# Low weight bits added as integers on GpSimd, and the gain of w_out multiplied there

## The chip, the cores and the metric

The kernel runs on one core of a Trainium2 chip. Its time is the device time of one execution in microseconds (us). Before the change three runs gave 670.62, 671.80 and 671.99 us, median 671.8 us. One more execution was taken with a profile; it took 670.49 us, of which the traced span is 668.7 us.

## The reference

Two stages follow each other. The first is a linear attention over 8 batches with 8 heads of 576 tokens and 64 columns; the second is a feed-forward block over 4608 tokens with 512 columns and 1024 hidden columns.

```
phi(x) = concat(exp(p - m), exp(m - p)),  p = x @ w_phi,  m = max |p| over features
num = phi(q) @ (phi(k)^T v);   den = phi(q) . sum(phi(k));   x = num / (den + 1e-6)
h = x @ w_in;  solu = h * softmax(h);  ln = (solu - mean) / sqrt(var + 1e-6) * g_ln
out = ln @ w_out
```

The inputs w_in (512 x 1024) and w_out (1024 x 512) arrive as 64-bit floats, the others as 32-bit floats.

## The kernel before

Attention runs over 16 units: a unit `u` is one batch and one half of its heads, and it has two parts (`sub`), each a pair of heads. Of a unit, TensorE projects keys (`pjk`) and queries (`pjq`), the middle tokens of both (`pjm`), VectorE takes the row maxima (`m`) and subtracts them (`dk`, `dq`), ScalarE takes both exponentials (`ek`, `fq`), TensorE forms the key-value product (`kvT`), the numerator (`num`) and the denominator (`den`), VectorE makes the reciprocal (`cmr`), and DMAs spread it over the partitions (`rb<-d`). GpSimd multiplies the numerator by it (`xa`, `xb`). For the first two units TensorE turns the queries (`dT`); for later units VectorE and two DMAs do.

The feed-forward block runs over 36 tiles of 128 tokens. The activations and the weights are split into a high and a low part, so that each product is three matmuls: `h` from `mxh`, `mxl` and `win_h`, `win_l` (24 matmuls of 512 columns a tile), and `o` from `uhs`, `uls` and `w_out_h`, `w_out_l` (24 more). GpSimd makes the low parts by subtraction.

The weights need work before that. There are eight weight tiles `i` of 128 x 1024: 0 to 3 are w_in, 4 to 7 are w_out. A tile comes from memory as pairs of 32-bit words (`wraw`, low and high word, 1 MB). `w_rebias` (ScalarE) puts the exponent of the high word in range. `w_bits` step 0 (VectorE) shifts the high word left by three into the 32-bit float `w`; step 1 (VectorE) shifts the low word right by 29 and ors its three bits in. For w_in, ScalarE then copies `win_h` and GpSimd subtracts to give `win_l`. For w_out, `w_gain` (ScalarE, two instructions a tile) multiplies by a column of g_ln, TensorE sums the tiles (`cmean`, then `cmall`), and GpSimd and ScalarE take the mean off and split the result (`w<-w,cms`, `w_out_h`, `w_out_l`).

No `h` matmul can start before all four `win_l` are there, and `cmean` needs all four gains of w_out. Both stand in TensorE's order within a few instructions of each other: `cmean`, one `pjk`, one `pjq`, `cmall`, and then the first `h`.

The order of all work is written out: `SEQUENCE` is a list of operation numbers, and every engine issues its share of it in that order, each with its own queue. An instruction that waits holds back all that stands behind it on its engine. The buffers (SBUF tags and eight PSUM banks, six of them single under tag `a`) are given out in the same order. The profile shows nearly all instructions under one helper line, so they are told apart by the names of their tiles.

Of the kernel before, what the change touches and what calls it, by code (L numbers as in the profile page):

```python
# [8 lines left out]
U32 = mybir.dt.uint32  # L9
AF = mybir.ActivationFunctionType  # L10
ALU = mybir.AluOpType
# [14 lines left out]
KV_PE = (0, 1)  # L26
SWITCH = 165.0
# [1285 lines left out]
```

## Time and profile before

| | before |
|---|---|
| median of three runs | 671.8 us |
| profiled execution | 670.49 us |
| its span | 668.7 us |
| TensorE (PE) busy | 660.4 us, 99% |
| VectorE (DVE) busy | 491.6 us, 74% |
| ScalarE (ACT) busy | 370.3 us, 55% |
| GpSimd (POOL) busy | 394.6 us, 59% |
| DMA, mean rate | 202 GB/s |

The shares are means over the whole span. The weights are prepared in its first 70 us, and there the engines stand otherwise: VectorE and the DMA engines are nearly full and GpSimd is mostly idle. The page's busy time of PE also holds short waits inside a matmul's modelled end, so the waits of PE are read from the view of waits and from start times in the timeline. PE's granted clock is 1.00 over the span but for its last stretch.

### The profile page before, as it was taken

How to read it: one execution, taken by the hardware profiler on the slowest of the kernel's cores; microseconds unless marked ns; L12 is line 12 of the kernel's file. 1: busy time of each engine (PE TensorE's matmuls, PEld its weight loads, DVE VectorE, ACT ScalarE, POOL GpSimd, SP SyncE). 2: the span in 40 equal slices, each digit the busy share in tenths (PEclk: the TensorE clock that was granted, in tenths of full speed). 3: DMA queues.
4: the chain of work that ended last, by engine and by line, in shares of the span. 5: the costliest groups of instructions: out<-in, count | busy, mean ns of one | idle time of the engine just before them, and what ended most of it. 6: DMA issues, size and time to landing. Idle time of an engine off the chain costs nothing.

```text
span 668.7 us, 13163 instructions
## 1 busy us (share of the span) xinstructions
PE 660.4 (99%) x4932; PEld 493.9 (74%) x4932; DVE 491.6 (74%) x754; ACT 370.3 (55%) x717; POOL 394.6 (59%) x438
## 2 busy tenths in 40 slices
PE   8999999999999999999999999999999899999998
PEld 6776667677777777777768777787777677788887
DVE  6999888878987697797788888589675746533440
ACT  4888874566465565455664576364545563331322
POOL 0125998786675574677593955845857555554501
PEclk9999999999999999999999999999999999999999
DMA  7897888777765695887685667764874663532302
GB/s 269 303 310 230 277 215 237 220 223 243 243 192 185 217 292 191 238 260 221 191 262 158 202 210 215 263 189 124 259 218 144 213 206 92 183 113 85 104 16 80
DMA packets 131280, 135.31 MB, mean 202 GB/s; under 512 B 55568, under 2 KB 105104, under 8 KB 130704
## 3 DMA queue, kind: packets, MB, share of 16 engines
q1 hardware_dynamic: 131216, 134.46, 65.1%
q8 instruction: 39, 0.64, 0.4%
q14 instruction: 25, 0.20, 0.1%
HBM read 85.53 MB, written 48.91 MB: 201 GB/s over the span
## 4 chain that ended last, share of the span: by engine, by line
PE 86%; DVE 9%; DMA 2%; issue 1%; POOL 1%; ACT 0%; SPq 0%; DVEq 0%; POOLq 0%; ACTq 0%
PE o L258 29%; PE h L258 28%; PE kvT L258 11%; PE num L258 6%; PE pjq L258 4%; PE pjk L258 4%; PE den L258 3%; DVE m L258 2%; DVE dq L258 2%; DVE w L258 2%; DVE dk L258 1%; PE pjm L258 1%; DMA out<-os 1%; DMA rb<-d 1%; DVE dE L258 0%
## 5 line engine op out<-in xcount | busy, mean ns | idle before, releaser
L258 POOL TENSOR_TENSOR uls<-uTs,uhs 128x1024 fp32r<-128x1024 f32 x33 | 78.9, 2391 | 46.4 <-ACT uhs L258 34.9
L258 PE MATMUL o<-w_out_h,uhs 128*128 128x512 f32 x264 | 103.9, 393 | 0.0
L258 PE MATMUL o<-w_out_h,uls 128*128 128x512 f32 x264 | 102.8, 389 | 0.0
L258 PE MATMUL o<-w_out_l,uhs 128*128 128x512 f32 x264 | 102.8, 389 | 0.0
L258 ACT ACTIVATE ek<-dk 128x512 f32<-128x512 f32 (+1 forms) x160 | 88.8, 587 | 18.8 <-DVE dk L258 15.5
L258 POOL TENSOR_TENSOR zt<-ek 128x512 f32<-128x512 f32 x52 | 68.2, 1311 | 48.8 <-ACT ek L258 48.3
L258 PE MATMUL h<-win_h,mxh 128*128 128x512 f32 x288 | 91.9, 400 | 0.0
L258 ACT ACTIVATE fq<-pT 128x512 f32<-128x512 f32 (+1 forms) x140 | 74.1, 561 | 31.6 <-DMA pT<-dqd 21.3
L258 PE MATMUL h<-win_h,mxl 128*128 128x512 f32 x288 | 89.0, 390 | 0.5 <-POOL mxl L258 0.5
L258 PE MATMUL h<-win_l,mxh 128*128 128x512 f32 x288 | 89.0, 390 | 0.0
L258 DVE TENSOR_REDUCE nm<-h 128x1 f32<-128x1024 f32 x36 | 43.8, 1218 | 60.0 <-PE h L258 60.0
L258 ACT ACTIVATE eu<-h,nm 128x1024 f32<-128x1024 f32 x36 | 40.1, 1113 | 59.9 <-DVE nm L258 52.3
L258 PEld LDWEIGHTS h<-win_h,mxh 128*128 128x128 f32 x288 | 52.0, 188 | 15.4 <-issue 1.4
L258 PEld LDWEIGHTS h<-win_h,mxl 128*128 128x128 f32 x288 | 54.0, 188 | 12.4 <-POOL mxl L258 0.9
L258 PEld LDWEIGHTS h<-win_l,mxh 128*128 128x128 f32 x288 | 54.1, 188 | 11.6
L258 PE MATMUL kvT<-ek,rawv 128*64 128x256 f32 x512 | 62.0, 383 | 0.0
L258 DVE SCALAR_TENSOR_TENSOR qz<-fq,kvf,qz 128x576 f32<-128x576 f32 x46 | 44.2, 972 | 21.1 <-ACT qz L258 21.1
L258 PEld LDWEIGHTS o<-w_out_h,uhs 128*128 128x128 f32 x264 | 49.6, 188 | 11.7 <-issue 0.5
L258 PEld LDWEIGHTS o<-w_out_h,uls 128*128 128x128 f32 x264 | 49.6, 188 | 10.4
L258 PEld LDWEIGHTS o<-w_out_l,uhs 128*128 128x128 f32 x264 | 49.6, 188 | 10.0
L258 PE MATMUL num<-fq,kvf 128*64 128x448 f32 (+1 forms) x304 | 56.5, 499 | 0.0
L258 ACT ACTIVATE qz<-fq,kvf 128x576 f32<-128x576 f32 x46 | 34.6, 770 | 38.2 <-DMA kvf<-dk 38.2
(109 smaller groups left out, 1278.1 us busy)
## 6 DMA issues: line engine op xcount, KB each, us to landing
du<-ub SPq DMA_DIRECT2D x33, 512.0 KB, 3.9
uTs<-du SPq DMA_DIRECT2D x33, 512.0 KB, 5.2
rb<-d SPq DMA_DIRECT2D x64, 144.0 KB, 3.9
dqd<-dq SPq DMA_DIRECT2D x14, 640.0 KB, 4.9
pT<-dqd SPq DMA_DIRECT2D x14, 640.0 KB, 5.9
out<-os SPq DMA_DIRECT2D x35, 256.0 KB, 4.1
rawq<-in_q SPq DMA_DIRECT2D x32, 256.0 KB, 4.2
rawk<-in_k SPq DMA_DIRECT2D x32, 256.0 KB, 5.0
```

The costliest lines, as they stand in the source:

```text
L258: return self.tc.keep_in_program_order(method(*args, **kwargs))
```

## The change

Three operations on the weights move, and the order of everything is new.

- The low bits are prepared apart from the float. For tiles 0 to 3 GpSimd takes the top byte of the low word, scales it by 1/32, limits it, and writes a whole number of 0 to 7 over the low word (`TENSOR_SCALAR wraw`). For tiles 4 to 7 VectorE shifts the low word right by 29 in place (`TENSOR_SCALAR wraw`). Neither needs the rebias of ScalarE.
- GpSimd adds that number to `w` as 32-bit integers (`TENSOR_TENSOR w<-w,wraw`, all eight tiles). VectorE's fused shift-and-or is gone.
- GpSimd multiplies w_out by the column of g_ln (`TENSOR_SCALAR w<-w,gcol`, two a tile). ScalarE's two multiplications a tile are gone.

```diff
+U8 = mybir.dt.uint8
+LOW_POOL = (0, 1, 2, 3)
 SEQUENCE = (
-    122, 2, 1, 123, 77, 124, 126, 125, 79, 86, 84, 312, 93, 127, 82, 80, 134, 88, 94, 83, 128, 87, 140, 137, 81,
...
     def w_bits(i, step, tag):
         raw = W["raw", i]
         lo, hi = raw[:, :, 0], raw[:, :, 1]
-        if step == 0:
+        if step == "hi":
             W[i] = sb(tag, [P, DF], U32, f"w32_{i}")
             nc.vector.tensor_scalar(out=W[i], in0=hi, scalar1=3, scalar2=None, op0=ALU.logical_shift_left)
+        elif step == "lo":
+            if i in LOW_POOL:
+                nc.gpsimd.tensor_scalar(
+                    out=lo, in0=lo.bitcast(U8)[:, :, 3], scalar1=1.0 / 32, scalar2=7.484375, op0=ALU.mult, op1=ALU.min
+                )
+            else:
+                nc.vector.tensor_scalar(out=lo, in0=lo, scalar1=29, scalar2=None, op0=ALU.logical_shift_right)
         else:
-            nc.vector.scalar_tensor_tensor(
-                out=W[i], in0=lo, scalar=29, in1=W[i], op0=ALU.logical_shift_right, op1=ALU.bitwise_or
-            )
+            nc.gpsimd.tensor_tensor(out=W[i], in0=W[i], in1=lo, op=ALU.add)
...
     def w_gain(i):
...
-            nc.scalar.activation(out=w, in_=w, func=AF.Copy, scale=gcol[:, f : f + 1])
+            nc.gpsimd.tensor_scalar(out=w, in0=w, scalar1=gcol[:, f : f + 1], scalar2=None, op0=ALU.mult)
```

On GpSimd all of the new work stands before the first `mxl`, the low part that the first `h` needs. Before, this is all that GpSimd had from the end of its set-up to that point:

```order
L258 TENSOR_TENSOR win_l<-w_0_490,win_h 128x1024
L258 TENSOR_TENSOR xa<-E,rb 128x576
L258 TENSOR_TENSOR win_l<-w_1_431,win_h 128x1024
L258 TENSOR_TENSOR xa<-E,rb 128x576 x2
L258 TENSOR_TENSOR win_l<-w_3_760,win_h 128x1024
L258 TENSOR_TENSOR xa<-E,rb 128x576
L258 TENSOR_TENSOR win_l<-w_2_995,win_h 128x1024
L258 TENSOR_TENSOR mxl<-xa,mxh 128x512
```

After the change, these are the last twelve rows of the same stretch, with twelve more ahead of them (of the numbers in the names, the first is the weight tile):

```order
L261 TENSOR_SCALAR wraw_609<-wraw_609 128x1024
L261 TENSOR_TENSOR w_6_776<-w_6_776,wraw_542 128x1024
L261 TENSOR_TENSOR xa<-E,rb 128x576
L261 TENSOR_TENSOR w_2_811<-w_2_811,wraw_609 128x1024
L261 TENSOR_TENSOR xa<-E,rb 128x576
L261 TENSOR_TENSOR w_5_910<-w_5_910,wraw_626 128x1024
L261 TENSOR_TENSOR win_l<-w_3_661,win_h 128x1024
L261 TENSOR_SCALAR w_5_910<-w_5_910,gcol 128x512 x2
L261 TENSOR_SCALAR w_6_776<-w_6_776,gcol 128x512 x2
L261 TENSOR_TENSOR xa<-E,rb 128x576 x2
L261 TENSOR_TENSOR win_l<-w_2_811,win_h 128x1024
L261 TENSOR_TENSOR mxl<-xa,mxh 128x512
```

The conversion and the add that the last `win_l` needs, and the gains that `cmean` needs, now stand in GpSimd's queue among the four `xa`.

VectorE starts the program in another order. Before, its first rows behind the memset were these (`m<-pjq`, `dq` are the first query group, whose two `dq` feed the first two `dT` of TensorE):

```order
L258 TENSOR_REDUCE m<-pjq 128x4 x2
L258 TENSOR_TENSOR dq<-pjq,m 128x512 x2
L258 TENSOR_REDUCE m<-pjk 128x4 x2
L258 TENSOR_TENSOR dk<-pjk,m 128x512 x2
L258 TENSOR_REDUCE m<-pjm 128x2 x2
```

Now, behind one `m<-pjq`, they are:

```order
L261 TENSOR_TENSOR dq<-pjq,m 128x512
L261 TENSOR_REDUCE m<-pjq 128x4
L261 TENSOR_REDUCE m<-pjk 128x4 x2
L261 TENSOR_TENSOR dk<-pjk,m 128x512 x2
L261 TENSOR_REDUCE m<-pjm 128x2
L261 TENSOR_TENSOR dk<-pjm,m 128x128
L261 TENSOR_TENSOR dqm<-pjm,m 128x128
L261 TENSOR_REDUCE m<-pjm 128x2
L261 TENSOR_REDUCE m<-pjk 128x4
L261 TENSOR_TENSOR dk<-pjm,m 128x128
L261 TENSOR_REDUCE m<-pjk 128x4
L261 TENSOR_TENSOR dq<-pjq,m 128x512
```

The first `dq` moved ahead of the second `m<-pjq`, and the second `dq` moved behind the key group and the middle tokens.

ScalarE casts the first `win_h` earlier. Before, the cast stood here, behind work of the second unit:

```order
L258 ACTIVATE fq<-dT 128x512
L258 ACTIVATE ek<-dk 128x4x128
L258 ACTIVATE fq<-dT 128x2x64 x2
L258 COPY E<-num 128x288
L258 CAST win_h<-w_1_431 128x1024
```

Now it stands right behind the first `kvf`, ahead of the middle queries of the first unit:

```order
L261 ACTIVATE wraw_240<-wraw_240 128x1024
L261 COPY kvs<-kvT 128x384
L261 ACTIVATE fq<-dT 128x512 x2
L261 COPY kvf<-kvt 128x384
L261 CAST win_h<-w_0_315 128x1024
```

The cast reads `w` as GpSimd's add leaves it, and the last `fq` that the first `den` needs stand behind it. TensorE's matmuls are the same in number and kind, 3380 of them in the program, and the same set of them stands ahead of the first `h`; only their order differs.

## Rows read from the trace of the kernel before

**Rows 1.** The page, busy time and share of each engine.
```profile
PE 660.4 (99%) x4932; PEld 493.9 (74%) x4932; DVE 491.6 (74%) x754; ACT 370.3 (55%) x717; POOL 394.6 (59%) x438
```

**Rows 2.** Waits of PE, whole span: total us, times, longest us.
```profile
PE den L258 <- DVE qz L258: 2.0, 1, 2.0
...
PE dT L258 <- DVE dq L258: 1.1, 1, 1.1
PE h L258 <- POOL mxl L258: 0.5, 1, 0.5
```

**Rows 3.** Two stretches: length, busy PE, PEld, DVE, ACT, POOL, clock, DMA share, GB/s.
```profile
10.00:55.00 45.00, 45.00 (x614) 32.24 (x610) 44.30 (x80) 38.55 (x78) 8.02 (x4) 1.00 0.92 310
55.00:70.00 15.00, 14.30 (x186) 8.83 (x185) 14.93 (x26) 12.11 (x21) 9.20 (x6) 1.00 0.78 228
```

**Rows 4.** Chain that ended last, first 75 us: start, us, what.
```profile
8.57 1.20 DVE m L258 x2
...
10.97 0.66 DVE m L258 x2
11.63 0.20 DVE dqm L258
...
56.05 4.60 DMA rb<-d
...
68.24 1.26 POOL mxl L258
```

**Rows 5.** Timeline, first 70 us: start, us, engine, operation, idle before.
```profile
8.12 0.63 PE L258 MATMUL dT<-ident,dq 128*128 128x128 f32 x4 [1.12 <-DVE dq L258]
...
12.73 1.95 PE L258 MATMUL kvT<-ek,rawv 128*64 128x256 f32 x16
...
17.26 1.18 ACT L258 ACTIVATE wraw<-wraw 128x1024 f32<-128x1024 f32 x1 [0.87 <-DMA wraw<-in_w_in]
...
61.42 2.63 PE L258 MATMUL cmean<-w,mean 128*32 128x512 f32 x16
...
68.46 0.62 PE L258 MATMUL h<-win_l,mxh 128*128 128x512 f32 x2
...
69.55 0.73 PE L258 MATMUL h<-win_h,mxl 128*128 128x512 f32 x2 [0.47 <-POOL mxl L258]
```

**Rows 6.** Groups by shape, whole span: busy us, mean ns of one, idle before.
```profile
L258 DVE SCALAR_TENSOR_TENSOR w<-wraw,w 128x1024 uint32<-128x1024 uint32 x8 | 9.7, 1221 | 0.1
L258 DVE TENSOR_SCALAR w<-wraw 128x1024 uint32<-128x1024 uint32 x8 | 5.7, 711 | 0.0
L258 ACT ACTIVATE w<-w,gcol 128x512 f32<-128x512 f32 x8 | 5.3, 730 | 0.0
L258 POOL COPY pm<-pT 128x128 f32<-128x128 f32 x14 | 4.1, 292 | 0.0
```

**Rows 7.** Groups of GpSimd by shape, first 70 us.
```profile
L258 POOL TENSOR_TENSOR win_l<-w,win_h 128x1024 fp32r<-128x1024 f32 x4 | 9.5, 2376 | 29.3 <-ACT win_h L258 29.3
L258 POOL TENSOR_TENSOR xa<-E,rb 128x576 f32<-128x576 f32 x4 | 6.1, 1528 | 21.5 <-DMA rb<-d 21.5
...
L258 POOL MEMSET spread<- 128x128 f32 x1 | 0.2, 205 | 0.0
...
L258 POOL MEMSET mean<- 128x32 f32 x1 | 0.1, 125 | 0.0
```

**Rows 8.** Timeline around 50, 345 and 521 us, VectorE and GpSimd.
```profile
48.54 2.39 POOL L258 TENSOR_TENSOR win_l<-w,win_h 128x1024 fp32r<-128x1024 f32 x1
...
50.57 0.92 DVE L258 TENSOR_SCALAR w<-wraw 128x1024 uint32<-128x1024 uint32 x1
...
345.02 2.39 POOL L258 TENSOR_TENSOR uls<-uTs,uhs 128x1024 fp32r<-128x1024 f32 x1
345.65 4.26 DVE L258 SCALAR_TENSOR_TENSOR qz<-fq,kvf,qz 128x576 f32<-128x576 f32 x2 [0.72 <-ACT qz L258]
...
521.36 1.53 DVE L258 SCALAR_TENSOR_TENSOR qz<-fq,kvf,qz 128x576 f32<-128x576 f32 x2
```

More of the change, by code (lines that the diff above doesn't have):

```diff
@@ L438, in linear_attention_then_moe @@
         op(("ws", i), "scalar", 1055, z, w_rebias, (i,), [("wl", i)], tiles=R4)
-        op(("wb", i, 0), "vector", 600, z, w_bits, (i, 0, w_tag[i]), [("ws", i)], [(w_tag[i], T)], R4)
-        op(("wb", i, 1), "vector", 1135, z, w_bits, (i, 1, None), [("wb", i, 0)], tiles=R4 + [T])
+        op(("wb", i, "hi"), "vector", 680, z, w_bits, (i, "hi", w_tag[i]), [("ws", i)], [(w_tag[i], T)], R4)
+        op(("wb", i, "lo"), "gpsimd" if i in LOW_POOL else "vector", 680, z, w_bits, (i, "lo", None), [("wl", i)], tiles=R4)
+        op(("wb", i, 1), "gpsimd", 2400, z, w_bits, (i, 1, None), [("wb", i, "hi"), ("wb", i, "lo")], tiles=R4 + [T])
         if i < 4:
@@ L444, in linear_attention_then_moe @@
         else:
-            op(("wg", i), "scalar", 1260, z, w_gain, (i,), [("wb", i, 1), "gain"], tiles=[T])
+            op(("wg", i), "gpsimd", 2400, z, w_gain, (i,), [("wb", i, 1), "gain"], tiles=[T])
     for r in range(2):
```

254 rows, old and new, of the table SEQUENCE are left out of this document.

## The prediction

> **What bounds the kernel now.** The page comes first: PE is busy 99% of the span, no other engine over 74% [rows 1]. A full TensorE is only a bound if it does not wait inside that time, so the view of waits comes next. Over 668.7 us it names three waits of PE that could go: 2.0 us of one `den` for VectorE, 1.1 us of the first `dT` for VectorE, 0.5 us of the first `h` for GpSimd [rows 2]. The work on TensorE is the same before and after, in number, kind and clock. So a gain can come only from waits, 3.6 us by that view; a loss has no such bound.
>
> The change touches the weights, so the stretch that matters is the one ahead of the first `h`, and there the table of stretches shows something that the means hide. From 10 to 55 us PE is busy all the time, VectorE 44.30 of 45 us, the DMA engines 92%, ScalarE 38.55 us, and GpSimd 8.02 us [rows 3]. The chain of waits runs through VectorE until it reaches the last `rb<-d` at 56.05 us, and from there through GpSimd to `mxl` [rows 4]. At 68.46 us TensorE has issued the second pair of matmuls of the first `h`, and the pair that needs `mxl` starts at 69.55 us, 0.5 us after the one ahead of it is done [rows 2, 5]. Three engines and the DMA arrive at the first `h` nearly together: taking load off one of them opens little, putting load on the fourth can close much.
>
> **The change part by part.** All of it lies ahead of the first `h`, and the sum is made against the profiled execution: span 668.7 us, 670.5 us in all. The median of the three runs is 671.8 us, 1.3 us above it.
>
> VectorE loses 8 fused operations of 1.22 us, 9.7 us, and gets 4 shifts of the low word. Their form writes every second word, which the shift of the high word does not; between the 0.71 us of that one and the 1.22 us of the fused one [rows 6] they cost 2.8 to 4.9 us. I take 2.8, the nearest form. VectorE is freed of 6.9 us. As TensorE is busy all through that stretch, this does not come out as time; it loosens the chain.
>
> ScalarE loses 8 multiplications of 0.73 us, 5.3 us in its groups [rows 6]. It was not full; worth nothing by itself.
>
> GpSimd gets 8 integer adds, 4 conversions of low bits and 8 multiplications by a column. No integer add stands in the trace; the nearest row is a two-input operation of the same size at 2.38 us [rows 7]: 19.0 us. The other two have one input. From above they are bounded by two-input operations of their size, 2.38 us and 1.26 us [rows 4, 7]. From below: a copy of 128 columns takes 0.29 us [rows 6], and two memsets give 0.83 ns for each further column ((205 - 125) / 96 [rows 7]), so 1.04 us for 1024 columns and 0.61 us for 512. Conversions: 4.2 to 9.5 us; multiplications: 4.9 to 10.1 us. I take the lower ends, from the one-input rows. Together 28.1 us, at most 38.6.
>
> The sum of GpSimd's line: before the first `mxl` it had four `win_l`, 9.5 us, and four `xa`, 6.1 us [rows 7], then `mxl`, 1.3. Now 45.0 to 55.5 us must fit between the landing of the first w_in tile, 17.26 us [rows 5], and the end of `mxl` at 69.5 us [rows 4]: 52.2 us. At my value 7.2 us are left for waits on loads, on VectorE's high words and on `rb`; at the upper end 3.3 us are missing. So I cost it at nothing, hidden behind TensorE's 68 us ahead of `h`, and that cover is thin.
>
> GpSimd's page gives a figure for the two kinds. The Trainium skill ("GPSIMD Engine Reference", Engine selection) says that two-input elementwise work is about twice as slow there as on VectorE and that one-input work runs near one element a cycle; at its 1.2 GHz that would be an estimate of 0.85 us and 0.43 us plus a start, close to my lower ends, so by the page the sum is near 45 us.
>
> The start of the program changes too. In steps of the chain, an operation of 512 columns takes 0.60 us, one of 256 takes 0.33, one of 128 takes 0.20 [rows 4]. The key maxima at 8.57 us stood behind four of the first kind, so VectorE begins at 6.17 us. The first `dq` is now one step earlier, so the first `dT` starts 0.6 us earlier than 8.12 us. The second `dq` stands behind nine steps of 0.60, two of 0.33 and three of 0.20: 6.7 us, done at about 13.5 us. The second `dT` ended before at 12.73 us, where the first `kvT` starts [rows 5]; now it can start only at 13.5 and end at 14.1. The first `kvT` comes 1.3 to 1.4 us later, and TensorE has nothing else in its order ahead of it.
>
> Sum: start +1.3; the wait at the first `h`, -0.5 if GpSimd is in time; loosened VectorE between 14 and 60 us, 0 to -1; everything after 70 us is reordered with no change of load, where the one wait of 2.0 us at `den` may go and another may come: 0. That makes -0.2 to +0.8 against 670.5, around 671; held against the median, around 672. I say 671.5 us: no change that can be measured (0.2%, 1.3 us, is about what three runs of this kernel can tell).
>
> **The rivals.** *VectorE's relief and the new order pay.* For it: the chain runs on VectorE for 55 us, and an engine that is 98% full delays what stands behind it. If the second `dT` is held up by something else anyway, the waits at `h` and at `den` go, and the start gives its 0.6 us, that is 0.5 + 2.0 + 0.6 below 671.5: 668.4 us. Against it: TensorE names only 3.6 us of waits in all.
>
> *GpSimd becomes the bound of the first `h`.* Place: the gains of the last two w_out tiles, which stand among the last rows ahead of `mxl`; `cmean` needs them and started at 61.42 us [rows 5], and TensorE can do only one `pjk` and one `pjq` between it and the first `h`. It decides once the added work passes 52.2 - 16.9 = 35.3 us with no waits, or less with them. At the upper end the line is late by 3.3 us, and with 2 us of waits for loads `h` starts about 5 us late: 675 to 677 us. For it: two-input times for the multiplications would be enough. Against it: the one-input rows.
>
> *VectorE and GpSimd hold each other up.* At 50.57 us a shift on VectorE took 0.92 us where the mean is 0.71 [rows 6], while a `win_l` ran on GpSimd until 50.93; at 345.65 us two `qz` took 4.26 us beside `uls`, and at 521.36, beside nothing, 1.53 [rows 8]. GpSimd was idle through most of the weights before; now it is busy some 45 of 52 us, and 12 shifts on VectorE fall into that time. If each waits for half of a 2-us operation with a chance of 0.86, that is 0.86 us each, 10 us, more than the 6.9 saved: VectorE is then 3.4 us fuller than before and TensorE waits for it: 675 us. At the 0.21 us of the one shift that met GpSimd it is 2.5 us, and the relief stays at 4.4. The Trainium skill ("SBUF — State Buffer", SBUF: two separate sides) says why: a VectorE operation that uses two ports and any GpSimd operation take an exclusive lock, and whichever comes second blocks for the whole instruction. The three rows agree with it.
>
> **How the numbers follow.** No change 0.36 (own range 670.2 to 672.8), relief 0.31, GpSimd late 0.19, mutual blocking 0.14. Of the first, about 0.02 falls below and 0.01 above the bound of 0.2%: faster 0.33, same 0.33, slower 0.34. The range reaches to both sides: down to 667, a little below the relief case, and up to 677, the upper end of a late GpSimd.
>
> **What would show it.** Right: the first `h` pair with `mxl` starts between 67 and 71 us, the one-input operations of GpSimd take 0.6 to 0.7 and 1.0 to 1.1 us, the first `kvT` starts near 14 us, and PE's named waits stay under 5 us. The relief case: first `h` by 67 us and no wait of `den` over 1 us. GpSimd late: PE waits at `cmean` or at `h` for POOL by 2 us or more, with GpSimd busy without a gap from 30 us on. Mutual blocking: VectorE's shifts have a mean over 1.2 us and PE waits for `dq` or `dk`. Wrong altogether: a wait of several us after 100 us, where the load did not change.

## The result and the profile after

The changed kernel takes 680.8 us (median of 4 runs, 680.3 to 682.5) against 671.2 us for the kernel before on the same chip: ratio 1.0148, interval 1.0123 to 1.0174. On a second chip the ratio was 1.0193 (1.0171 to 1.0216). It is slower, by 10 to 13 us, where no change was forecast. One run of e8 (827.62 us, granted clock 0.754) and one of e15 (922.72 us, 0.669) are left out of the times below, as their clock was far under that of the others. The profiled execution took 681.2 us with a span of 679.4 us, 10.7 us more than before.

The page answers to [rows 1]: PE is as full as before in share, and GpSimd has 50 us more, 49 of them ahead of the first `h` (66.1 against 16.7 us of work, in the table of all kernels below). The two lower lines are GpSimd's busy tenths in 40 slices of 17 us, before and after.

```profile
PE 666.3 (98%) x4932; PEld 495.5 (73%) x4932; DVE 494.1 (73%) x750; ACT 366.2 (54%) x709; POOL 444.4 (65%) x458
...
POOL 0125998786675574677593955845857555554501
POOL 2999989974867565856685873683849546652500
```

The same two stretches as in [rows 3], with the stretch from 10 to 30 us ahead of them:

```profile
10.00:30.00 20.00, 17.11 (x231) 12.38 (x231) 18.10 (x31) 15.20 (x29) 15.62 (x6) 1.00 0.89 305
...
10.00:55.00 45.00, 41.56 (x556) 28.89 (x558) 42.92 (x71) 37.30 (x73) 40.16 (x15) 1.00 0.88 295
55.00:70.00 15.00, 11.69 (x100) 6.93 (x99) 13.74 (x23) 6.60 (x13) 14.92 (x8) 0.96 0.63 182
```

TensorE now stands 3.4 us from 10 to 55 us, where it was full, and 3.3 us from 55 to 70 us (0.7 before); GpSimd goes from 8 to 40 us in the longer stretch. Its groups up to 85 us (answering to [rows 7]):

```profile
L261 POOL TENSOR_TENSOR w<-w,wraw 128x1024 uint32<-128x1024 uint32 x8 | 20.1, 2513 | 0.2
L261 POOL TENSOR_SCALAR wraw<-wraw 128x1024 uint32<-128x1024 uint8 x4 | 16.0, 4000 | 12.4 <-DMA wraw<-in_w_in 12.2
L261 POOL TENSOR_SCALAR w<-w,gcol 128x512 f32<-128x512 f32 x8 | 13.2, 1664 | 0.2
L261 POOL TENSOR_TENSOR win_l<-w,win_h 128x1024 fp32r<-128x1024 f32 x4 | 9.9, 2480 | 0.0
L261 POOL TENSOR_TENSOR xa<-E,rb 128x576 f32<-128x576 f32 x4 | 6.0, 1519 | 0.0
```

Read the last column: once the first weights have landed GpSimd hardly waits (0.7 us in all). The new operations take 20.1 + 16.0 + 13.2 = 49.3 us, where 28.1 were predicted and 38.6 was the upper end. The timeline shows where this line begins, what hangs on it and where it ends (GpSimd, with the VectorE, ScalarE and TensorE operations that matter):

```profile
14.22 7.79 POOL L261 TENSOR_SCALAR wraw<-wraw 128x1024 uint32<-128x1024 uint8 x2 [12.18 <-DMA wraw<-in_w_in]
...
43.08 2.40 POOL L261 TENSOR_TENSOR w<-w,wraw 128x1024 uint32<-128x1024 uint32 x1
...
43.42 2.61 DVE L261 TENSOR_SCALAR wraw<-wraw 128x1024 uint32<-128x1024 uint32 x1
...
60.14 0.40 ACT L261 COPY E<-num 128x288 f32<-128x288 f32 x1 [3.13 <-POOL xa L261]
...
63.87 0.70 ACT L261 COPY E<-num 128x288 f32<-128x288 f32 x2 [2.79 <-POOL xa L261]
...
68.49 6.19 POOL L261 TENSOR_SCALAR w<-w,gcol 128x512 f32<-128x512 f32 x4
74.65 2.78 POOL L261 TENSOR_TENSOR xa<-E,rb 128x576 f32<-128x576 f32 x2
...
79.73 1.28 POOL L261 TENSOR_TENSOR mxl<-xa,mxh 128x512 fp32r<-128x512 f32 x1
...
81.06 0.73 PE L261 MATMUL h<-win_h,mxl 128*128 128x512 f32 x2 [0.38 <-POOL mxl L261]
```

From 14.22 us to the end of `mxl` at 81.01 GpSimd has 66.1 us of work and 0.7 us of gaps. The first `h` pair with `mxl` starts at 81.06 us instead of 69.55: 11.5 us late. From there to the end of the span are 598.34 us, before 599.15. So the whole loss lies ahead of the first `h`, and the rest gives 0.8 us back.

PE's named waits (answering to [rows 2]) don't show GpSimd as the cause; the longest are these:

```profile
PE kvT L261 <- ACT E L261: 1.5, 2, 1.4
...
PE kvT L261 <- ACT ek L261: 1.1, 1, 1.1
PE pjm L261 <- ACT fq L261: 0.9, 1, 0.9
...
PE h L261 <- POOL mxl L261: 0.4, 1, 0.4
```

The link is in the timeline above: ScalarE's copy into `E` waits 3.13 and 2.79 us for an `xa` on GpSimd, since `xa` is what reads `E` and frees its buffer. TensorE then waits for ScalarE. By the time `h` comes, the lateness has already been passed on, and only 0.4 us are left to be seen at `h`.

### The profile page after: what moved, and what is told of

It reads as the page before. It is cut to its first block, busy times and chain, and to the rows that moved or that the text cites. A ratio compares the mean times of both kernels' runs of the same rounds, so it can differ in the third digit from the quotient of the medians.

```text
span 679.4 us, 13175 instructions
## 1 busy us (share of the span) xinstructions
PE 666.3 (98%) x4932; PEld 495.5 (73%) x4932; DVE 494.1 (73%) x750; ACT 366.2 (54%) x709; POOL 444.4 (65%) x458
## 4 chain that ended last, share of the span: by engine, by line
PE 86%; DVE 5%; POOL 5%; issue 1%; DMA 1%; ACT 1%; SPq 0%; DVEq 0%; ACTq 0%; POOLq 0%
PE o L261 29%; PE h L261 29%; PE kvT L261 11%; PE num L261 6%; PE pjk L261 3%; PE pjq L261 3%; PE den L261 3%; POOL w L261 2%; POOL wraw L261 1%; DVE m L261 1%; DMA wraw<-in_w_in 1%; PE pjm L261 1%; POOL xa L261 1%; DVE dk L261 1%; DVE wraw L261 1%
## 5 line engine op out<-in xcount | busy, mean ns | idle before, releaser
L261 POOL TENSOR_TENSOR uls<-uTs,uhs 128x1024 fp32r<-128x1024 f32 x33 | 80.3, 2434 | 57.2 <-PE o L261 21.6
L261 ACT ACTIVATE ek<-dk 128x512 f32<-128x512 f32 (+1 forms) x160 | 89.5, 583 | 28.9 <-DVE dk L261 20.1
L261 ACT ACTIVATE fq<-pT 128x512 f32<-128x512 f32 (+1 forms) x140 | 75.4, 560 | 17.9 <-DMA pT<-dqd 11.5
L261 PE MATMUL kvT<-ek,rawv 128*64 128x256 f32 x512 | 64.2, 389 | 1.8 <-ACT E L261 1.4
L261 DVE TENSOR_TENSOR eu<-h,eu 128x1024 f32<-128x1024 f32 x36 | 43.6, 1212 | 16.3 <-ACT eu L261 13.5
```

The source lines that it names most:

```text
L261: return self.tc.keep_in_program_order(method(*args, **kwargs))
```

## The experiments

Theory 1: GpSimd's line, dearer than thought, sets the first `h`. Theory 2: VectorE and GpSimd stop each other. Theory 3: the new order costs by itself. The first four kernels are the changed kernel with parts undone. The numbers of all runs stand in one table behind the last experiment.

**e1, conversions back to VectorE.**
```
-LOW_POOL = (0, 1, 2, 3)
+LOW_POOL = ()
```


> The changed kernel with the four conversions of the low bits taken off GpSimd: all eight are shifts on VectorE (12 shifts become 16... four of 711 ns each come back to VectorE, 2.8 us). Theory 1 (the chain of GpSimd work ahead of the first h sets the loss): GpSimd's line loses 4 x 4.00 = 16.0 us, more than the 11.5 us by which the first h is late, so the first h comes between 69 and 72 us and the time is 669 to 673 us. Theory 2 (VectorE and GpSimd hold each other up, and TensorE waits for VectorE): the shifts on VectorE beside GpSimd's additions only grow in number, so most of the loss stays, 677 to 682 us. Theory 3 (the new order itself costs): 679 to 682 us.

**e2, multiplications back to ScalarE.**
```
-            nc.gpsimd.tensor_scalar(out=w, in0=w, scalar1=gcol[:, f : f + 1], ..., op0=ALU.mult)
+            nc.scalar.activation(out=w, in_=w, func=AF.Copy, scale=gcol[:, f : f + 1])
```


> The changed kernel with the eight multiplications by g_ln back on ScalarE (5.8 us there in the kernel before). Theory 1: GpSimd's line loses 13.2 us, again more than the 11.5 us by which the first h is late; the first h comes between 69 and 73 us, the time is 669 to 674 us. Theory 2: the blocking by additions and conversions stays, the time is 676 to 681 us. Theory 3: 679 to 682 us.

**e3, both (only the additions stay on GpSimd).**

> Both undone: only the eight integer additions (20.1 us) stay on GpSimd, in the new order, with the unfused shifts on VectorE. Theory 1: GpSimd's line ends well before the first h needs it; first h at 69 to 70 us, time 669 to 672 us, no better than the better of the two single undoings by more than 2 us. Theory 2: the eight additions beside VectorE's shifts still block, 672 to 677 us. Theory 3: 679 to 682 us.

**e4, none of the moved work on GpSimd, new order.** The fused shift-or of before stands where the addition stood, the multiplication is ScalarE's.

> Nothing on GpSimd: the fused shift-or on VectorE and the multiplication on ScalarE as in the kernel before, in the new order. Theories 1 and 2: the time of the kernel before within 2 us, 669 to 673 us. Theory 3 (the new order costs by itself): above 676 us.

Measured: 677.4, 675.9, 677.8 and 682.2 us, before 670.4. Each theory fails in part. Taking 12 to 28 us off GpSimd brings the first `h` from 81.1 to between 74.9 and 77.4 us and not to 70, and GpSimd then has gaps of 5 to 18 us: another bound lies at about 75 us. The trace of e2 shows it (VectorE's fourth reciprocal, then the `xa` that uses it):

```profile
61.57 0.22 DVE L261 RECIPROCAL cmr<-dE 128x9 f32<-128x9 f32 x1
...
69.86 1.40 POOL L261 TENSOR_TENSOR xa<-E,rb 128x576 f32<-128x576 f32 x1 [4.75 <-DMA rb<-d]
```

The last `xa` waits 4.75 us for the DMA that brings `rb`, and `rb` comes from the last `cmr`. Behind that `xa` stand the last `win_l` and `mxl`, so the first `h` pair with `mxl` starts 13.3 us after the `cmr`. In e3 it is the same, with `cmr` at 62.41 us, a wait of 4.33 us for `rb` and 13.3 us to `h`. Before, that `cmr` started at 54.72 us and its `xa` did not wait for `rb`. By the same 13.3 us, an estimate from e2 and e3, the first `h` of the changed kernel, with its `cmr` at 62.45 us, could come at about 75.7 us; it comes at 81.06, and GpSimd's line adds these last 5.3 us. In e1 the last `xa` does not wait for `rb`, and its 77.4 us are not taken apart.

And e4 is as slow as the change with none of the moved work on GpSimd. Its last `cmr` comes at 69.20 us, and `h` 13.1 us behind it. Its VectorE operations on the weights, put where the additions stood, take 21.4 us against 15.4 before, and its granted clock is 0.83 from 10 to 20 and from 30 to 40 us, where it was 1.00 before; what of its 12 us is due to each and what to the order, e4 doesn't tell.

**e5 and e6, the order of before.** All moved operations (e5), and the additions alone (e6), in the order of the kernel before.

> All three operations moved as in the changed kernel, but in the order of the kernel before (each conversion or unfused shift stands behind its weight's upper shift, the additions and multiplications where the or and the multiplication stood). Theory 1 (GpSimd's line sets the first h): 49.3 us of new GpSimd work and 16.9 us of old still stand ahead of the first h, which comes at 79 to 84 us; 677 to 682 us. Theory 3 (the new order costs, about 4 us of TensorE waits before 30 us and more up to 80): those waits go and with them the loss, 669 to 673 us. Both together, each with its part: 675 to 678 us.

> Only the eight integer additions on GpSimd, unfused shifts on VectorE, multiplication on ScalarE, in the order of the kernel before. Theory 3 (what was left of the loss with the same operations in the new order, 677.8 us, is the order's): 669 to 672 us. Theory 2 (additions on GpSimd beside VectorE's shifts hold each other up): 674 to 678 us. Theory 1 says nothing against 669 to 672 us, as 20 us fit into GpSimd's idle time.

Measured: 697.6 and 679.8 us. So with all operations moved the new order is better than the old one by some 17 us (697.6 against 680.8). It does cost at the start. PE's busy time from 10 to 30 us is 20.00 us before, 20.00 in e5, 19.82 in e6, but 17.11 in the changed kernel and 16.98 to 17.82 in e1 to e4, whatever operations are moved. In e6 a further thing is seen: a shift on VectorE that begins beside an addition lasts until about half a microsecond after the addition ends (the second pair below), and the 16 shifts take 23.7 us.

```profile
44.82 5.23 POOL L257 TENSOR_TENSOR w<-w,wraw 128x1024 uint32<-128x1024 uint32 x2 [14.21 <-DVE wraw L257]
...
45.24 2.53 DVE L257 TENSOR_SCALAR w<-wraw 128x1024 uint32<-128x1024 uint32 x1
47.70 2.93 DVE L257 TENSOR_SCALAR wraw<-wraw 128x1024 uint32<-128x1024 uint32 x1
```

**e7, the operations by themselves.** A kernel of its own, described in its expectation.

> Not the computation: the kernel writes zeros and only runs GpSimd's new operations twice each, alone, with variants (multiplier a number, a column, a row of equal entries; conversion with one operation, from packed bytes; addition from packed words), and then beside a row of VectorE shifts and beside a row of VectorE operations out of PSUM. If the durations in the changed kernel (conversion 4.00 us, multiplication 1.66 us, addition 2.51 us) are GpSimd's own price, they stand alone too, within a tenth; if they come from sharing with VectorE, alone the conversion takes at most 2.4 us and the multiplication at most 1.3 us, and beside VectorE's shifts they are longer by more than a third.

GpSimd alone (`pair` is the conversion, two of its four with one operation; `pa<-pa,pair` the addition; `pa<-pa,gcol` the multiplication, as TENSOR_SCALAR by the column and as TENSOR_TENSOR with the column read as a second tensor, the same entry all along a row; `pa<-pa` an f32 TENSOR_SCALAR with two operations; groups as above):

```profile
L132 POOL TENSOR_SCALAR pair<-pair 128x1024 uint32<-128x1024 uint8 x4 | 13.1, 3284 | 0.3
L132 POOL TENSOR_SCALAR pb<-flat 128x1024 uint32<-128x1024 uint8 x2 | 7.3, 3626 | 0.1
L132 POOL TENSOR_SCALAR pa<-pa 128x1024 f32<-128x1024 f32 x2 | 7.2, 3624 | 0.1
L132 POOL TENSOR_SCALAR pa<-pa,gcol 128x1024 f32<-128x1024 f32 x2 | 5.7, 2842 | 0.2
L132 POOL TENSOR_TENSOR pa<-pa,pair 128x1024 uint32<-128x1024 uint32 x2 | 4.7, 2372 | 0.2
...
L132 POOL TENSOR_SCALAR pa<-pa,gcol 128x512 f32<-128x512 f32 x2 | 3.1, 1562 | 2.2 <-DVE pa L132 2.1
...
L132 POOL COPY pb<-pa 128x1024 f32<-128x1024 f32 x2 | 2.4, 1210 | 0.1
L132 POOL TENSOR_TENSOR pa<-pa,gcol 128x512 f32<-128x512 f32 x2 | 2.1, 1039 | 0.2
```

The durations in the changed kernel are, within a tenth, GpSimd's own price: the conversion with both operations takes 3.71 us alone (first pair of the four), 4.00 in the kernel; the multiplication 1.56 and 1.66; the addition 2.37 and 2.51. A copy of the same size takes 1.21 us, so TENSOR_SCALAR takes 2.3 times (one operation) to 3 times (two) as long as the copy, and longer than an operation on two tensors. Packed bytes make little difference (3.63). Beside a row of VectorE shifts the three take 4.36, 2.01 and 2.69 us; beside VectorE operations that read PSUM 3.76, 1.57 and 2.38.

**e8 and e11, idle additions in the kernel before** (the same kernel twice; the profile of e11 is the one shown).
```
+            if i in (0, 1, 3, 4, 7):
+                nc.gpsimd.tensor_tensor(out=lo, in0=W[i], in1=lo, op=ALU.add)
```


> The kernel before, with nothing moved, and five GpSimd additions of 128x1024 integers added to it, right behind the VectorE or of the weights 0, 1, 3, 4 and 7; they write words that nothing reads any more, into GpSimd's idle time between 24 and 50 us. Theory 2 (a GpSimd operation on two tensors stops VectorE's operations from SBUF until it ends; VectorE has no reserve there): shifts and ors of VectorE stretch by 1 to 2 us each beside them, VectorE is 3 to 7 us later at 50 us and the time is 672 to 677 us. If the loss comes only from waiting for the result of the additions, from the order or from GpSimd's late end: 669 to 671.5 us.

> The same kernel as with the five idle additions before, for a profile at TensorE's full clock. Theory 2: 678 to 684 us again, with shifts and ors of VectorE that last until the addition beside them ends (2.3 to 3.4 us in place of 0.69 and 1.22 us), and TensorE waiting for VectorE's results between 28 and 75 us.

**e12, idle conversions in the same places** (`tensor_scalar` as in the change, instead of the addition).

> The kernel before with five idle conversions (the one-tensor form, 3.7 us each alone) in the places where the idle additions (two tensors, 2.4 us) stood. If VectorE is stopped by GpSimd's operations on two tensors (theory 2 in its narrow form): beside a conversion a shift is slowed at the start of it only, the loss is at most a third of that of the additions, 669 to 674 us, though GpSimd is busy longer. If any occupation of GpSimd costs (a late GpSimd line, or memory shared by any two operations): 680 to 688 us.

Measured: 680.0 us for e8 (before 669.7), 681.9 for e11 and 680.7 for e12 (before 668.6). Five additions that nobody needs cost 10 to 13 us, in GpSimd's idle time; but conversions, which let VectorE's shifts through for most of their length, cost 12 us too. So theory 2 falls as the main reason here. The profile of e12 gives another:

```profile
45.25 10.72 POOL L258 TENSOR_SCALAR wraw<-wraw 128x1024 uint32<-128x1024 uint8 x2 [11.78 <-DVE w L258]
...
62.27 1.40 POOL L258 TENSOR_TENSOR xa<-E,rb 128x576 f32<-128x576 f32 x1
...
63.69 0.40 ACT L258 COPY E<-num 128x288 f32<-128x288 f32 x1 [11.67 <-POOL xa L258]
```

The first `xa` starts at 62.3 us (46.99 before) because it stands in GpSimd's queue behind the idle work, which itself waits for VectorE's ors; ScalarE's copy into `E` waits 11.67 us for it, and PE 9.3 us for that copy.

**e15 and e16, the five additions split** into those with no `xa` close behind them (`i in (0, 1)`) and those with (`i in (3, 4, 7)`).

> The kernel before with idle additions behind the weights 0 and 1 only, where GpSimd has nothing to do until 31 us and no xa until 47 us. If what costs is an xa that stands in GpSimd's queue behind the idle work: 669 to 671.5 us, though one shift of VectorE lasts 2.6 us in place of 0.7. If stopped VectorE operations decide: two fifths of the loss of the five, 673 to 676 us.

> The kernel before with idle additions behind the weights 3, 4 and 7 only, with xa behind them in GpSimd's queue. If the queue decides: nearly all of the 12 us, 678 to 682 us, and ScalarE's copy into E waits for xa by 5 us or more. If stopped VectorE operations decide: three fifths, 675 to 678 us.

Measured: 671.4 (ratio 1.001, 0.998 to 1.004) and 677.7 us (1.011, 1.005 to 1.017), before 669.7. The two cost nothing that can be told, though one shift lasts 2.60 us; the three cost 8 us, and ScalarE's copy waits 6.72 us for `xa`, where the queue's side had forecast 5 us or more. The time itself does not decide: 677.7 us lies in the range given for stopped VectorE operations and just under that for the queue. So the place in GpSimd's queue costs, as the wait shows; how much of the 8 us is due to VectorE operations that last longer was not taken apart.

**e9, a cheaper multiplication, same place and order.**
```
-            nc.gpsimd.tensor_scalar(out=w, in0=w, scalar1=gcol[:, f : f + 1], ..., op0=ALU.mult)
+            nc.gpsimd.tensor_tensor(out=w, in0=w, in1=gcol[:, f : f + 1].to_broadcast([P, DM]), op=ALU.mult)
```


> The changed kernel with one edit: the eight multiplications on GpSimd take the column of g_ln as a second tensor with equal entries in a row (alone 1.04 us) in place of a number for each partition (alone 1.57 us). Place, order and result are the same. Theory 1 (GpSimd's line sets the first h): GpSimd's line is 8 x 0.5 = 4 us shorter, the first h 3 to 5 us earlier than 81 us, and the time 676 to 678.5 us. Theory 2: the form on two tensors stops VectorE's shifts as the additions do, which takes back part of it, 678 to 681 us. Theory 3: 680 to 682 us.

In the profiled execution theory 1 holds to a few tenths: GpSimd's work falls from 66.1 to 62.2 us, the first `h` comes 4.7 us earlier (0.7 of it from an earlier landing), the profiled time is 677.5 us. The other three runs took 679.3 to 682.5 us at a mean clock of 0.992 to 0.994, and the median, 680.8 us, lies above the forecast of 676 to 678.5 us and shows no gain that can be told.

```profile
75.08 1.28 POOL L261 TENSOR_TENSOR mxl<-xa,mxh 128x512 fp32r<-128x512 f32 x1
...
76.41 0.73 PE L261 MATMUL h<-win_h,mxl 128*128 128x512 f32 x2 [0.37 <-POOL mxl L261]
```

**e10, old order up to about 20 us, new order behind.**

> The changed kernel with the steps up to about 20 us in the order of the kernel before and all others in the new order. Theory 3 for the start (the new order makes TensorE wait 4 us more before 30 us, with or without the moved operations): these waits go, the excess before 30 us falls from 8.8 to 5 to 6 us. If the first h is set by TensorE's progress too, the time is 676.5 to 679 us; if by GpSimd's line alone, which starts at the landing of the weights and not at TensorE's progress, the first h stays at 80 to 82 us and the time at 679.5 to 682 us.

685.9 us. The waits before 20 us went, but where the two orders meet TensorE waits 5 us for a `dk` at 30 us, and the weights land 2.7 us later than in the changed kernel, so GpSimd's line starts at 16.9 us and, with its 66.8 us, ends at 85.5. Both forecasts missed, and a clean price of the start this is not.

**e13, no shifts on VectorE,** with **e14,** the change again, for comparison. e13 leaves the shifts out, so its additions read two raw words of one tile.
```
-            nc.vector.tensor_scalar(out=W[i], in0=hi, scalar1=3, ..., op0=ALU.logical_shift_left)
-                nc.vector.tensor_scalar(out=lo, in0=lo, scalar1=29, ..., op0=ALU.logical_shift_right)
-            nc.gpsimd.tensor_tensor(out=W[i], in0=W[i], in1=lo, op=ALU.add)
+            nc.gpsimd.tensor_tensor(out=W[i], in0=hi, in1=lo, op=ALU.add)
```


> The changed kernel without VectorE's twelve shifts of the weights (left out; the additions read the raw words). GpSimd's line keeps all its operations. Theory 1: GpSimd's line is only as much shorter as it was stretched (conversions 3.7 in place of 4.0 us, additions 2.4 in place of 2.5 us), the first h still at 76 to 80 us and the time 676 to 680 us. Theory 2: TensorE's waits for VectorE and, behind it, ScalarE between 20 and 68 us go, and the time is 668 to 674 us.

> The changed kernel as it is, as the control for the kernels of this group: 680 to 682 us, as measured.

675.7 and 681.8 us, so between the two forecasts. In e13 GpSimd again has no gap worth naming, and its line is shorter than I had reckoned, as the additions in their new form take 1.89 us and nothing is stretched:

```profile
L261 POOL TENSOR_SCALAR wraw<-wraw 128x1024 uint32<-128x1024 uint8 x4 | 15.4, 3858 | 11.7 <-DMA wraw<-in_w_in 11.5
L261 POOL TENSOR_TENSOR w<-wraw 128x1024 uint32<-128x1024 uint32 x8 | 15.1, 1893 | 0.2
L261 POOL TENSOR_SCALAR w<-w,gcol 128x512 f32<-128x512 f32 x8 | 12.4, 1564 | 0.2
```

The first `h` pair with `mxl` moves with the end of that line again, to 73.7 us.

The profiled executions side by side, without e7 and e8 (e11 is the kernel of e8); GpSimd's line is from its first operation after 5 us to the end of the first `mxl`, and `h` is the start of the first `h<-win_h,mxl`, all from timelines, in us. The time is the median of the runs, the last column the kernel before on the same chip.

| kernel | line starts | work | gaps | h | span - h | time | before |
|---|---|---|---|---|---|---|---|
| before | 31.3 | 16.7 | 21.5 | 69.6 | 599.2 | 671.2 | |
| changed | 14.2 | 66.1 | 0.7 | 81.1 | 598.3 | 680.8 | 671.2 |
| e14, the same | 13.2 | 66.1 | 0.7 | 80.0 | 600.4 | 681.8 | 668.6 |
| e1 | 21.0 | 51.6 | 4.8 | 77.4 | 597.8 | 677.4 | 670.4 |
| e2 | 13.6 | 54.0 | 7.3 | 74.9 | 600.0 | 675.9 | 670.4 |
| e3 | 20.1 | 37.9 | 17.7 | 75.7 | 600.4 | 677.8 | 670.4 |
| e4 | 23.7 | 18.1 | 40.4 | 82.3 | 598.0 | 682.2 | 670.4 |
| e5 | 17.3 | 65.9 | 9.7 | 94.7 | 600.7 | 697.6 | 670.0 |
| e6 | 24.5 | 37.5 | 17.3 | 79.4 | 599.5 | 679.8 | 670.0 |
| e9 | 13.6 | 62.2 | 0.6 | 76.4 | 599.3 | 680.8 | 669.7 |
| e10 | 16.9 | 66.8 | 1.9 | 85.6 | 598.3 | 685.9 | 669.7 |
| e11 | 25.6 | 33.0 | 19.7 | 80.3 | 598.0 | 681.9 | 668.6 |
| e12 | 25.7 | 39.0 | 15.9 | 82.6 | 597.7 | 680.7 | 668.6 |
| e13 | 13.5 | 58.8 | 1.4 | 73.7 | 600.8 | 675.7 | 668.6 |
| e15 | 25.7 | 21.5 | 24.6 | 71.8 | 598.3 | 671.4 | 669.7 |
| e16 | 44.3 | 26.7 | 4.9 | 77.9 | 598.4 | 677.7 | 669.7 |

In all sixteen the span behind the first `h` is 597.7 to 600.8 us. What a profiled execution of this group takes is decided, to within these 3 us, by when its first `h` comes. In e5, e11, e12 and e16 `mxl` ends about 2 us before that `h`: there TensorE is late by itself, through what it waited for earlier.

## Why the prediction was wrong

**The step that failed** is the price of the two one-tensor kinds on GpSimd: "I take the lower ends, from the one-input rows." The conversions came to 16.0 us where 4.2 were taken and 9.5 was the upper end, the multiplications to 13.2 where 4.9 were taken and 10.1 was the end. Together 20.1 us of the 21.2 by which the new work was short (49.3 - 28.1); the additions, taken from the row of their own form, were short by 1.1. The row chosen was that of another instruction, a copy; and "bounded from above by two-input operations of their size" was argued, not read. e7 shows both wrong: TENSOR_SCALAR costs more than TENSOR_TENSOR there. The Trainium skill's rule that I set beside it ("GPSIMD Engine Reference", Engine selection; one input near line rate) gave 0.85 and 0.43 us plus a start by estimate. The runs show 3.71 and 1.56 alone, and the measurement decides.

**A second step failed beside it:** VectorE in the new order was put at +1.3 us for the start and 0 to -1 for its relief. The last `cmr` ahead of the first `h` comes 7.7 us later instead (before, then changed):

```profile
54.72 0.21 DVE L258 RECIPROCAL cmr<-dE 128x9 f32<-128x9 f32 x1
...
62.45 0.21 DVE L261 RECIPROCAL cmr<-dE 128x9 f32<-128x9 f32 x1
```

Through `rb` that alone would put the first `h` at about 75.7 us, 6 us late. So right prices on GpSimd alone would hardly have saved the forecast: e2, with VectorE's work as in the changed kernel and 7.3 us of gaps in GpSimd's line, is still 5.5 us slower than the kernel before, and e3, with 37.9 us of work in that line where 45.0 were forecast, but four more shifts on VectorE, 7.4 us. What makes that `cmr` late is only partly known: in e13, without the shifts on VectorE, it comes at 57.76 us, 3.7 us earlier than in e14 on the same chip; the rest stays open.

**The mechanism was named, as a rival.** "GpSimd becomes the bound of the first `h`" had its threshold (35.3 us of added work, passed by 14), its place ahead of `mxl` and a chance of 0.19, and in the changed kernel it is what sets the first `h`. It was priced at 675 to 677 us with the same terms that were too small. Right arithmetic with the measured terms: the line has 66.8 us, gaps included, from 14.2 us on and ends at 81.0, against 69.5 before, 11.5 us; less 0.8 us given back later, that is the 10.7 us of the span. The window was larger than I took it, since the weights land at 14.2 us in the new order and not at 17.26. Shorter lines bear it out: in e9 (3.9 us less work) no gap opens, in e13 (7.3 us less) 0.7 us more, and the first `h` comes earlier by the rest and by the earlier start. Only e9 changes GpSimd's work alone; e13 frees VectorE too.

**Its sign was partly wrong.** I looked for PE waiting 2 us or more at `cmean` or `h` for GpSimd. In the old order it does (e5: 15.5 us at `cmean`); in the changed kernel it comes through `xa`, `E` and ScalarE, a path that the prediction did not have. "GpSimd busy without a gap from 30 us on" was right, from 14 us on.

**VectorE, freed of 6.9 us:** not so. Its 12 shifts took 10.7 + 5.6 = 16.3 us, the 16 operations of before 15.4. At the 0.69 us that a shift takes alone they are 8.3; 8 us went into standing beside GpSimd, against the 10 that the rival "hold each other up" reckoned. Half of its sign came out: the shifts have a mean of 1.36 us, over the 1.2 named, but PE's waits for `dq` and `dk` sum to only 1.5 us. Its mechanism is there (43.42 us above: a shift that begins beside the addition and ends 0.55 us after it). On GpSimd it stretches the line by about 3 us (4 x 0.29 + 8 x 0.10 + 8 x 0.14); on VectorE it probably has a share in the late `cmr`, which no run gives by itself; and e15 shows that a stopped shift alone need not cost. The rule of the Trainium skill cited there ("SBUF — State Buffer", SBUF: two separate sides) agrees for additions. Beside a conversion of 4.37 us in e7, though, shifts in its middle took 0.69 us, and 1.45 us at its start and end, so not every GpSimd operation holds the lock throughout.

**The start, +1.3:** first `kvT` at 14.82 us, 14.1 forecast, as it also waited 0.4 us for the DMA of `rawv`. But it didn't end there: PE's busy time from 10 to 30 us is 2.9 us shorter, and 1.7 to 3.0 us shorter in every kernel with the new order at the start. In the changed kernel this is hidden behind GpSimd's line. Whether it has a share in the late `cmr` is not shown.

**Right:** nothing lost behind the first `h`; the wait of 2.0 us at `den` gone. That ScalarE's relief is worth nothing no run shows by itself.

## What to carry to other kernels

Price an operation on an engine from a row of the same instruction there; a copy and a TENSOR_SCALAR of one size differ by 2.3 to 3 times on GpSimd. When taking work off the bound does not bring the whole loss back, look for the wait that then ends last: here it was the DMA of `rb`, behind a late `cmr` on VectorE. An engine's idle time is not free where its queue also holds a short operation that others wait for: ask what stands behind the new work in the queue (here `xa`, which frees `E`), not only whether the sum fits. And where all that follows has nearly a fixed length, as here behind the first `h` (to within 3 us), one start time measures every variant.

## What the hardware showed that was not expected

A GpSimd multiplication by a column costs less when the column is given as a second tensor (1.04 us) than as a number for each partition (1.56 us), at 128x512 in e7.

TensorE's clock fell once. In the changed kernel TensorE stood still for about 1 us at 65 us and worked at nearly the lower level (1.2 GHz; the granted clock has a mean of 0.58) in the four us from 68 on, by estimate 1.7 us of work lost (4 x 0.42). That this lengthened the execution is not shown: the first `h` still waited for `mxl`. The stretches around it (columns as in the stretches above):

```profile
64.00:68.00 4.00, 2.61 (x21) 1.39 (x18) 3.49 (x7) 4.00 (x9) 4.00 (x2) 1.00 0.79 240
68.00:72.00 4.00, 4.00 (x28) 2.00 (x30) 1.69 (x4) 0.20 (x1) 4.00 (x4) 0.58 0.96 282
```
